# TensorE's order in the last three heads of an attention-decode block: the maxima of single heads before older value passes, the last group's turn before the last maxima

## The chip, the cores and the metric

The kernel runs on one core of a Trainium2 chip. The metric is device time in microseconds (us) of one launch. The engines are called PE (TensorE, matrix multiplication), DVE (VectorE), ACT (ScalarE), POOL (GpSimd) and SP (SyncE, which here only issues DMA transfers). Each engine works through its own list of instructions in order; between engines there are semaphores. A time printed as "at 638.5" is counted from the start of the span of the profiled execution.

## The reference, cut to what matters

One token passes through a transformer block whose layer norms are modulated by a vector `c`: attention over a cache of 16384 keys and values with 32 heads of 128, then a gated feed-forward network (FFN) with inner size 1728. The model width is 640. All inputs are bfloat16.

```python
mod = (silu(c) @ w_mod).reshape(1, 6, 1, 640)
sa, ca, ga, sb, cb, gb = (mod[:, i] for i in range(6))
h = layernorm(x) * (1 + ca) + sa
# attention A: Hq = Hkv = 32, Sk = 16384, Dh = 128
q = (h @ wq).reshape(1, 1, 32, 128)
scores = einsum('bhqd,bhkd->bhqk', q, k_cache) * 128 ** -0.5
p = softmax(scores)
o = einsum('bhqk,bhkd->bhqd', p, v_cache)
x = x + ga * (o.reshape(1, 1, 4096) @ wo)
# FFN B: F = 1728
h = layernorm(x) * (1 + cb) + sb
x = x + gb * ((silu(h @ w_gate) * (h @ w_up)) @ w_down)
```

The keys and the values are 32 x 4 MB each. They, `wo` and the FFN weights are read once, so about 290 MB pass from memory into the core.

## The kernel before, in words

**How operations get their order.** The kernel is written as a plan. Each operation is given an engine, a position (a number that looks like a time in us) and the operations it depends on. At the end every engine's operations are sorted by position and written out as that engine's list; where a dependency crosses engines a semaphore wait is put in front of the operation. A wait holds all that stands behind it on the same engine. DMA transfers are operations of SP, so their order is the order of positions on SP.

**Units.** Keys are treated in units (`UNITS`): 15 pairs of heads (units 0 to 14, heads 0 to 29), and then head 30 alone (unit 15) and head 31 alone (unit 16). `NU` is 15, `H` is 32. `BU(u)` and `EU(u)` are the planned begin and end of a unit: unit 15 has 614.0 and 632.6, unit 16 has 633.8 and 652.4. `B` and `E` in the loop stand for these; `TL` is `BU(16)`.

**Scores, on DVE.** For each unit DVE multiplies the keys in place with the broadcast query in two halves (L577, `mult`), adds halves together three times (L597, `fold`), reduces the rest to scores in `S_sb` (L599, `red`) and takes the maximum of each partition (L601, `max`, into `pm`).

**Maxima and softmax.** `stage_top` (L461) turns the partition maxima into one number. PE transposes `pm` into a row (L464, called row15 and row16 below for the last two units), DVE takes the maximum of the row (L466, top15 and top16), PE broadcasts it to all partitions (L474), and ACT scales it (L478, `nb`). `softmax` then has ACT write the exponentials (L496 for a single head, into `P_sb`). The two DVE steps of a unit's maximum stand in the DVE list between the two multiplications of the next unit: the list is mult of unit 16, first half; top15; mult of unit 16, second half; folds; red16; max16; top16.

**Values, on PE.** `value(h)` (L523) is one pass of 32 matmuls (L529) over the 4 MB of values of head `h`, called pv28, pv29 and pv30 below. It depends on the exponentials of that head and on the landing of its values. ACT copies the result into the head's four rows of `acc_sb` (L540). When all heads of a group are there, `diag` (L543, matmuls L547) turns the group's rows into columns; for the last group it is diag7 and covers heads 28, 29 and 30. Head 31 has another form: 128 small matmuls (L631, pv31 below), in three parts as its values land in three parts of 2, 1 and 1 MB. `sums` (L513) adds the exponentials and inverts the sum (L515 on PE, two ACT operations).

**Behind the heads.** The product with `wo` (L670) takes 155 small matmuls for heads 0 to 30 and five more for head 31; then come the residual and the second layer norm, `gate` and `up` (L733, 140 matmuls), `down` (L751, 70 matmuls in three parts as its weights land), and the output.

**SP's list at the end.** Values of head 30 (waits for pv28, whose slot of `vring` it takes), `wo` in three transfers, values of head 31 in three transfers (wait for pv29), then `w_gate`, `w_up` and five transfers of `w_down` (all wait for red16, since they take the slots of the last keys).

**PE's list at the end.** pv28; pv29; row15; the broadcast of top15; sums for heads 28 to 30; row16; the broadcast of top16; sums for head 31; pv30; diag7; `wo` for heads 0 to 30; pv31; and the rest as above.

## Time and profile before

| what | value |
|---|---|
| median of 3 runs | 692.49 us (692.16 to 694.05) |
| the profiled execution | 692.85 us |
| its span (first to last instruction) | 691.1 us |
| DVE busy | 612.9 us, 89% of the span |
| PE busy | 330.8 us, 48% of the span |
| ACT busy | 66.3 us, 10% of the span |
| memory read | 290.48 MB, 420 GB/s over the span |
| mean granted PE clock | 0.72 of full speed |

The span is what the profile's times refer to; the 1.75 us by which the profiled time is longer lie around it. The page gives for each engine its busy time; a view of stretches gives the same for any part of the span, with the granted clock and the busy share of the 16 DMA engines; the chain of waits follows the end of the span back, at each step to what released it; and the list of transfers gives for each issue the time until its data had landed.

### The profile page before, as it was taken

The page shows a single profiled execution, that of the slowest core. Times are in us where ns is not written, and L with a number is a line of the kernel's source. Part 1 is how long each engine was busy: PE and PEld are TensorE (multiplying, and loading weights), DVE is VectorE, ACT ScalarE, POOL GpSimd, SP SyncE. Part 2 cuts the span into 40 slices and gives each one's busy share as a digit, 9 for nine tenths or more (in the row PEclk, how much of TensorE's full clock was granted, in tenths as well). Part 3 has the DMA queues.
Part 4 walks back from the last instruction along what each step waited for, and adds up shares of the span by engine and source line. Part 5 has one row for each costly group of instructions (what it writes and reads, how often), then busy time and mean ns, then how long its engine had stood idle before and what let it go on. Part 6 is the DMA issues. An engine that isn't in the chain of part 4 may idle for free.

```text
span 691.1 us, 5975 instructions
## 1 busy us (share of the span) xinstructions
PE 330.8 (48%) x1946; PEld 137.7 (20%) x1946; DVE 612.9 (89%) x195; ACT 66.3 (10%) x210; POOL 0.2 (0%) x4
## 2 busy tenths in 40 slices
PE   2440270908164553719028644719082644737186
PEld 2210020303021111303003211203021211212056
DVE  3079999999999999999999999999999999996801
ACT  1020100001010101010011101010000101010000
POOL 0000000000000000000000000000000000000000
PEclk9985595867768685959559785958686775959565
DMA  9999999999999999999999999999999999999991
GB/s 394 417 442 425 436 439 425 458 403 448 421 436 424 465 408 427 451 421 432 424 438 434 450 408 429 453 419 439 421 459 412 450 413 435 430 427 417 417 415 64
DMA packets 11238, 290.68 MB, mean 421 GB/s; under 512 B 1046, under 2 KB 1752, under 8 KB 3928
## 3 DMA queue, kind: packets, MB, share of 16 engines
q1 hardware_dynamic: 11220, 290.48, 97.9%
q8 instruction: 10, 0.16, 0.1%
q14 instruction: 4, 0.03, 0.0%
q10 hardware_dynamic: 4, 0.00, 0.0%
HBM read 290.48 MB, written 0.00 MB: 420 GB/s over the span
## 4 chain that ended last, share of the span: by engine, by line
DMA 42%; DVE 36%; PE 20%; issue 1%; ACT 1%; SPq 0%; DVEq 0%
DMA vbig<-in_A_v_cache_dram 33%; PE psb L529 16%; DVE kbig L577 16%; DVE kbig L597 13%; DMA kbig<-in_A_k_cache_dram 5%; DMA x_row<-in_A_x_dram 4%; DVE S_sb L599 4%; DVE kbig L592 1%; PE psb L733 1%; PE psb L670 1%; PE psb L631 1%; ACT P_k L492 0%; PE psb L751 0%; DVE pm L601 0%; DVE gm L466 0%
## 5 line engine op out<-in xcount | busy, mean ns | idle before, releaser
L577 DVE TENSOR_TENSOR kbig<-kbig,qbc 128x8192 bf16<-128x8192 bf16 (+2 forms) x34 | 278.0, 8175 | 23.8 <-DMA kbig<-in_A_k_cache_dram 23.8
L529 PE MATMUL psb<-vbig,P_sb 128*4 128x512 bf16 (+1 forms) x992 | 258.1, 418 | 26.4 <-DMA vbig<-in_A_v_cache_dram 20.6
L597 DVE TENSOR_TENSOR kbig<-kbig 128x8192 bf16<-128x8192 bf16 (+3 forms) x50 | 238.3, 4766 | 1.7
L529 PEld LDWEIGHTS psb<-vbig,P_sb 128*4 128x4 bf16 (+1 forms) x992 | 88.2, 89 | 189.1 <-issue 85.3
L464 PE MATMUL psb<-ident_f,pm 128*1 128x128 f32 x34 | 9.6, 381 | 199.5 <-DVE pm L601 199.5
L599 DVE TENSOR_REDUCE S_sb<-kbig 128x256 f32<-128x4096 bf16 (+1 forms) x17 | 70.9, 4169 | 0.6
L540 ACT ACTIVATE acc_sb<-psb 4x512 f32<-4x512 f32 x31 | 18.2, 586 | 268.3 <-PE psb L529 268.3
L464 PEld LDWEIGHTS psb<-ident_f,pm 128*1 128x1 f32 x34 | 1.5, 81 | 204.5 <-DVE pm L601 204.2
L474 PE MATMUL psb<-gm,ones_f 1*64 1x1 f32 (+1 forms) x64 | 6.6, 254 | 57.3 <-DVE gm L466 57.3
L478 ACT ACTIVATE nb<-psb 128x1 f32<-128x1 f32 x17 | 2.9, 172 | 184.1 <-PE psb L474 183.9
L504 PE MATMUL psb<-P_k,place 128*128 128x128 bf16 x60 | 9.1, 308 | 22.9 <-ACT P_k L492 22.9
L474 PEld LDWEIGHTS psb<-gm,ones_f 1*64 1x64 f32 (+1 forms) x64 | 5.1, 203 | 63.5 <-DVE gm L466 63.5
L372 PE MATMUL psb<-vbig,h_col 128*128 128x512 bf16 x40 | 12.5, 484 | 10.0 <-DMA vbig<-in_A_wq_dram 10.0
L492 ACT ACTIVATE P_k<-S_sb,nb 64x256 bf16<-64x256 f32 x30 | 15.2, 506 | 0.9
L559 ACT ACTIVATE Z<-msk,on_f 128x16 bf16<-128x16 f32 (+1 forms) x28 | 6.4, 298 | 71.7 <-DVE on_f L554 71.7
L621 DVE TENSOR_TENSOR On<-psb,rl 128x3 bf16<-128x3 f32 x1 | 0.2, 165 | 13.0 <-PE psb L547 13.0
L547 PE MATMUL psb<-sel,acc_sb 128*128 128x4 f32 (+1 forms) x64 | 8.4, 255 | 5.4 <-ACT acc_sb L540 5.4
L466 DVE TENSOR_REDUCE gm<-psb 1x2 f32<-1x128 f32 (+1 forms) x17 | 4.6, 273 | 6.3 <-PE psb L464 6.3
L504 PEld LDWEIGHTS psb<-P_k,place 128*128 128x128 bf16 x60 | 5.2, 131 | 24.1 <-ACT P_k L492 24.1
L547 PEld LDWEIGHTS psb<-sel,acc_sb 128*128 128x128 f32 x64 | 7.7, 191 | 9.4 <-ACT acc_sb L540 9.4
L592 DVE TENSOR_TENSOR kbig<-kbig 128x8192 bf16<-128x8192 bf16 x2 | 8.8, 4424 | 0.1
L634 DVE TENSOR_TENSOR On<-psb,rl 128x1 bf16<-128x1 f32 x1 | 0.2, 160 | 9.7 <-PE psb L631 9.7
(96 smaller groups left out, 102.9 us busy)
## 6 DMA issues: line engine op xcount, KB each, us to landing
vbig<-in_A_v_cache_dram SPq DMA_DIRECT2D x31, 4096.0 KB, 29.3
kbig<-in_A_k_cache_dram SPq DMA_DIRECT2D x4, 4096.0 KB, 33.4
vbig<-in_A_wq_dram SPq DMA_DIRECT2D x1, 5120.0 KB, 25.7
kbig<-in_w_mod_dram SPq DMA_DIRECT2D x1, 4800.0 KB, 14.1
kbig<-in_A_wo_dram SPq DMA_DIRECT2D x1, 3840.0 KB, 22.5
kbig<-in_B_w_gate_dram SPq DMA_DIRECT2D x1, 2160.0 KB, 13.4
kbig<-in_B_w_up_dram SPq DMA_DIRECT2D x1, 2160.0 KB, 18.2
vbig<-in_A_v_cache_dram SPq DMA_DIRECT2D x1, 2048.0 KB, 18.3
```

The source lines that it names most:

```text
L372: last = e.matmul(q_ps[b][:, 0:n * 128], lhsT=h_col[:, k:k + 1].broadcast_to([128, 128]), rhs=wv[:, k, n0:n0 + n * 128], start=(k == 0), s ...
L464: o_T = op(PE, E + 0.1, lambda e: e.matmul(row_ps, lhsT=pm[:, u:u + 1], rhs=ident_f[:], start=True, stop=True), deps=[o_max[u], o_idf, lnl ...
L474: last = e.matmul(top_ps[w * hh:w * hh + w, :], lhsT=ones_f[0:1, 0:w], rhs=gm2[:, hh:hh + 1], start=True, stop=True)
L492: o_exp[h + hh] = op(ACT, pt + 0.2 + 0.01 * hh, lambda e, p_=p_, hh=hh: e.activation(out=P_k[p_], in_=S_sb[p_, :], func=ACTF.Exp, scale=SC ...
L504: last = e.matmul(R_ps[:, TT * hh:TT * (hh + 1)], lhsT=place[:, hh, eo, :], rhs=P_k[:, TT * eo:TT * (eo + 1)], start=(eo == 0), stop=(eo = ...
L529: return e.matmul(acc_ps[s2][0:4, :], lhsT=P_sb[:, s2, bass.ds(t, 4)], rhs=vbig[:, bass.ds(at, 512)], start=start, stop=stop)
L540: o_acc[h] = op(ACT, pos + 0.05, lambda e: e.activation(out=acc_sb[32 * j:32 * j + 4], in_=acc_ps[s2][0:4, :], func=ACTF.Copy), deps=[o_pv ...
L547: last = e.matmul(OT_ps[:, h0:h0 + n], lhsT=acc_sb[:, 128 * i:128 * (i + 1)], rhs=sel[:, i, 0:n], start=(i == 0), stop=(i == 3))
L577: prev.append(op(DVE, B + (13.0 if u == 0 else 4.5) * c, lambda e, ks=ks[:, a:b, :], qb=qb: e.tensor_tensor(out=ks, in0=ks, in1=qb, op=ALU ...
L592: prev[c] = op(DVE, B + 13.0 * c + 8.7, lambda e, ks=ks[:, a:b, :]: e.tensor_tensor(out=ks[:, :, 0:64], in0=ks[:, :, 0:64], in1=ks[:, :, 6 ...
L597: prev = [op(DVE, E - 14.0 + 0.1 * (8 - math.log2(w)), lambda e, ks=ks, w=w: e.tensor_tensor(out=ks[:, :, 0:w], in0=ks[:, :, 0:w], in1=ks[ ...
L599: o_red[u] = op(DVE, E - 4.0, lambda e, ks=ks, w=w, nt=nt: e.tensor_reduce(out=S_sb[:, 0:nt], in_=ks[:, :, 0:w], axis=AX.X, op=ALU.add), d ...
```

## The change

Three things are moved in the plan; no operation is added or removed.

- The value pass of head 29 takes position `E + 0.15` of unit 15, that is 632.75, where it had 618.7. Row15 stands at 632.7, so row15 now comes before pv29 in PE's list. The transfer of head 31's values, which waits for pv29, takes 633.1 where it had 620.2.
- The value pass of head 30 is placed at 638.3, directly behind the sums for heads 28 to 30, where it had 653.2. The transfer of its values keeps its position.
- diag7 takes `E + 0.15` of unit 16, that is 652.55, directly behind row16 (652.5) and before the broadcast of top16; it had 653.5.

PE's list at the end becomes: pv28; row15; pv29; the broadcast of top15; sums for heads 28 to 30; pv30; row16; diag7; the broadcast of top16; sums for head 31; `wo` for heads 0 to 30; pv31; and the rest as before. ACT's copies of the passes' results move with them: that of pv29 to 632.8, before `nb` of unit 15 as before, that of pv30 to 638.4, before `nb` of unit 16. The lists of DVE and SP keep their order.

```diff
@@ -583,11 +583,14 @@
                         value(hp, pt + 0.5)
                         if hp % GQ == GQ - 2:
                             sums(hp // GQ, pt + 0.6, hp - 2, GQ)
-                        value(hp + 1, pt + 0.7)
+                        value(hp + 1, pt + 0.7 if u < NU else E + 0.15)
                         if hp % GQ == GQ - 2:
                             diag(hp // GQ, pt + 0.8, hp - 2, GQ)
                     else:
                         sums(H, pt + 0.4, hp - 2, 3)
+                        load_v(hp, BU(NU) + 6.0)
+                        value(hp, pt + 0.5)
+                        diag(H // GQ - 1, E + 0.15, HD, H - 1 - HD)
...
         pt = softmax(NU + 1, EU(NU + 1) + 0.2)
-        load_v(H - 2, BU(NU) + 6.0)
         sums(H + 1, pt + 0.3, H - 1, 1)
-        value(H - 2, pt + 0.5)
-        diag(H // GQ - 1, pt + 0.8, HD, H - 1 - HD)
...
-        load_v(H - 1, BU(NU) + 6.2)
+        load_v(H - 1, EU(NU) + 0.5)
         s2 = (H - 1) % 2
```

## The prediction

> **What bounds the kernel now.** I read the chain of waits first, then the instructions in order of time over the last 100 us, then the stretches with the DMA share, then the transfers with their time to landing. The end of the chain, in columns start, length, what:

> ```profile
> 629.65 8.86 PE psb L529 x32
> 639.05 4.34 DVE kbig L577
> ...
> 653.78 0.30 DVE pm L601
> 654.12 0.60 PE psb L464 x2
> ...
> 657.02 9.22 PE psb L529 x32
> ...
> 667.96 4.10 PE psb L670 x155
> 672.07 0.51 PE psb L631 x19
> 672.57 2.17 issue
> 674.74 3.06 PE psb L631 x109
> ...
> 681.81 4.44 PE psb L733 x140
> 686.57 2.13 PE psb L751 x70
> ```

> Here the end is set by a dependency chain: pv29 (629.65 to 638.51), DVE's work on unit 16 until max16 (654.08), the softmax of head 31, pv30 (657.02 to 666.24), diag7, `wo`, pv31 with a pause of 2.17 us in which PE waited for nothing the profile shows, the second norm, gate and up, down. PE did next to nothing between 640.6 and 654, though pv30 could have run. DVE lost time too (start, length, engine, operation; in brackets the idle time before it and its releaser):

> ```profile
> 628.53 0.29 DVE L601 TENSOR_REDUCE pm<-S_sb 128x1 f32<-128x128 f32 x1
> ...
> 638.77 0.28 DVE L466 TENSOR_REDUCE gm<-psb 1x1 f32<-1x128 f32 x1 [5.61 <-PE psb L464]
> ```

> The partition maxima of head 30 were ready at 628.82, but row15 stood behind pv29, so top15, and behind it the second half of unit 16's multiplication, waited 5.61 us. Now the DMA side, as stretches (last two columns: busy share of the 16 DMA engines, GB/s):

> ```profile
> 638.00:654.00 16.00, 1.49 (x9) 0.76 (x7) 15.06 (x7) 1.63 (x6) 0.00 (x0) 0.59 1.02 419
> 654.00:662.00 8.00, 6.72 (x20) 2.64 (x21) 0.34 (x2) 1.04 (x5) 0.00 (x0) 0.53 0.99 411
> 668.00:672.00 4.00, 4.00 (x157) 4.00 (x154) 0.17 (x1) 0.00 (x0) 0.00 (x0) 0.54 1.02 412
> 672.00:676.00 4.00, 1.83 (x70) 1.77 (x68) 0.00 (x0) 0.00 (x0) 0.00 (x0) 0.50 1.04 391
> 676.00:678.00 2.00, 1.78 (x67) 1.70 (x64) 0.17 (x2) 0.00 (x0) 0.00 (x0) 0.50 0.33 112
> ```

> The DMA engines are full until 676 and done at 678: a second bound, close behind the first. The transfers give its landings (KB each, us from issue to landing):

> ```profile
> vbig<-in_A_v_cache_dram SPq DMA_DIRECT2D x1, 4096.0 KB, 13.6
> vbig<-in_A_v_cache_dram SPq DMA_DIRECT2D x1, 2048.0 KB, 18.3
> kbig<-in_B_w_gate_dram SPq DMA_DIRECT2D x1, 2160.0 KB, 13.4
> kbig<-in_B_w_up_dram SPq DMA_DIRECT2D x1, 2160.0 KB, 18.2
> kbig<-in_B_w_down_dram SPq DMA_DIRECT2D x1, 80.0 KB, 11.2
> ```

> With the issue times from the instructions in order of time (625.74, 638.54, 653.77, 654.19, 666.8): head 30's values land at 639.3; head 31's first half at 656.8 and its last quarter, issued at 639.9 with a median of 21.1 for the two quarters, near 661.8; w_gate at 667.2, w_up at 672.4, and the last piece of w_down at 678.0. Before, down began at 686.57, so all of this had landed 8.5 us early.

> **The change, part by part.** No instruction is added or removed; only waits move.

> (1) *Row15 ahead of pv29.* It may start at 628.87 (max15 ends at 628.82) and takes 0.58 us, as row16 did on an idle PE: done at 629.45. Pv29 waited for its values until 629.65 anyway, so the cost is 0, hidden by that landing. If max15 came later, each us would hold pv29, its copy, the broadcast of top15, and SP's transfer of head 31 with all FFN weights behind it; the cover is 0.2 us. A later issue of head 31's values would still cost no DMA time until the engines ran out of `wo`, whose last piece lands 24.2 us after its issue at 627.1, at 651.

> (2) *DVE.* top15 no longer waits: first half until 633.16, top15, second half until 637.8, folds 8.0 us, red16 (waits for head 30's exponentials, part 3, long done) and max16 end 5.6 us earlier, at 648.5. SP may issue the FFN weights at 648.2, not 653.77.

> (3) *Pv30 ahead of row16.* The broadcast of top15 still stands behind pv29: 638.55 to 638.95. ACT copies pv29's result until 639.15 as before, then `nb` 0.17 and the exponentials with their sum 0.5: 639.9. Sums on PE 0.4: 640.3. Head 30's values landed at 639.3, so pv30 starts at 640.35. Its length: 8.0 us (all at full clock, the pass at 591.1 to 599.1) to 13.7 us (32 matmuls at 0.427, the spacing at half clock). I take 9.2, the pass of before, since PE idles about 1 us between the passes: end at 649.6. The granted clock fell to 0.50 in the long pause before pv30 (0.50 from 642 to 654), so a colder start is possible. [...]

> (4) *Row16, diag7, the last softmax.* Row16 waits for PE, not for max16: 649.6 to 650.2. The copy of pv30 takes 0.59, diag7 1.05: 651.3. Top16 (0.28) runs on DVE beside diag7. Broadcast 0.58, `nb` 0.2, exponentials 0.5, sums 0.58: 653.3. Diag7 before the broadcast costs 0.8 us here and saves its 1.05 later. `wo` (4.1 to 4.2 us; weights there since 651): 657.5. Pv31 needs 0.51 + 3.06, and I keep the 2.17 us pause: 663.2, past the last landing of head 31 (661.8). Before, pv31 ended at 677.80; this chain is 14.6 us shorter. The way on to gate takes 4.0 us (677.80 to 681.81): gate at 667.2, just when w_gate lands.

> (5) *What takes over.* The transfers do not move. The same packets go through engines that were full from 626 to 676, in the same order on SP; issuing the FFN weights 5.6 us earlier only lengthens the queue. So w_up lands at 672.4, up needs half of 4.44: 674.6, the product 0.33: 674.95. The first two parts of down fit in before the last piece of w_down at 678.0. Then the last 20 of 70 matmuls, 2.13 x 20 / 70 = 0.61, with 0.05 to react: 678.66. From the end of down (688.70) to the end of the span (691.07) it took 2.37: span **681.05**, 10.0 us less than before. The chain of part 4 may be 4.7 us late (gate at 671.9) before it decides again.

> The profiled time is 1.78 above its span and 0.36 above the median of the runs: 681.05 + 1.78 - 0.36 = **682.5**.

> **Rivals.**

> *B. PE's chain still decides.* Pv30 wholly at half clock adds 4.5 us (13.7 for 9.2) and one more pause like the 2.17 us one, in gate or pv31 while DMA is full, makes 6.7; less the slack of 4.7 leaves 2.0: 684.5 (683.7 to 687). For it: the clock stood at 0.50 in most of the tail, and the pause was real. Against: pv29 runs directly before, and passes back to back took 8.0.

> *C. The transfers end sooner.* If the earlier issue let them finish 4.2 us sooner, the whole 14.6 would be gained: 692.5 - 14.6 = 677.9. Against: shares of 0.99 to 1.04 leave no hole to fill.

> *D. Slower: FFN weights share the queue with head 31.* They are now issued 13 us before head 31's last quarter lands, before it was 8. If the engines served them side by side, head 31's values would land only with everything else at 678.0; then the 128 matmuls, 0.51 + 3.06, end pv31 at 681.6 and the old way of 13.27 (677.80 to 691.07) follows: 694.9, time 696.3. It decides against the change once the first half lands after 674.2 (677.80 - 3.57). Against: w_gate was already issued while head 31 was pending, yet the landings kept the order of issue, w_up 5.2 us behind w_gate (2.2 MB at 420 GB/s). [...]

> *E. The edit does nothing:* pv30 or row15 finds a wait that I overlooked and the old chain stands, 692.5. Both inputs, max15 at 628.82 and head 30's landing at 639.3, speak against it.

> **How the numbers follow.** My forecast has 0.78, B 0.12, C 0.04, D 0.04, E 0.02. The forecast's own range is 681.6 to 683.6 (the last landing within 0.5 us either way, and 0.5 for a new set of runs, whose spread before was -0.3 to +1.6). Towards C I go down to 681.0, towards B up to 685.2, which takes in half of B; beyond lie about 0.18. A measurement can tell about 0.3% (2.1 us) from no change. Faster: 0.78 + 0.12 + 0.04 = 0.94; same: 0.02; slower: 0.04.

> **What would show it.** Right: row15 at 628.9 and pv29 still at 629.7; top15 with no wait; max16 at 648.5; pv30 from 640.4; w_up's landing near 672.4 as before; up waiting for a DMA, and the last part of down starting at the last landing, near 678. Wrong: a DMA share clearly under 1 between 626 and 676, a landing of head 31 later than 662, gate later than 671.9, or pauses on PE between 657 and 676 that sum to over 5 us.

## The result, and the profile after

The changed kernel takes 684.44 us in the median of 4 runs (684.22 to 684.49), the kernel before 692.65 in the same comparison: ratio 0.9878, 95% interval 0.986 to 0.9895. It is 8.2 us faster, where 10.0 had been forecast. Its profiled execution took 684.22 with a span of 682.4, 8.6 less than the span before. The forecast of 682.5 was 1.9 us too low; the range (681.0 to 685.2) holds the result.

The instructions of the changed kernel in order of time; columns start, length, engine, line, operation, and in brackets the idle time before it and what ended it. Lines between the two edits have moved by three, so L604 is the maximum that was L601:

```profile
628.73 0.58 PE L464 MATMUL psb<-ident_f,pm 128*1 128x128 f32 x2 [2.44 <-DVE pm L604]
629.49 8.33 PE L529 MATMUL psb<-vbig,P_sb 128*4 128x512 bf16 x32 [0.18 <-DMA vbig<-in_A_v_cache_dram]
632.92 0.27 DVE L466 TENSOR_REDUCE gm<-psb 1x1 f32<-1x128 f32 x1
...
639.53 7.81 PE L529 MATMUL psb<-vbig,P_sb 128*4 128x512 bf16 x32
...
647.92 0.29 DVE L604 TENSOR_REDUCE pm<-S_sb 128x1 f32<-128x128 f32 x1
...
650.97 3.77 PE L670 MATMUL psb<-A_sb,kbig 128*128 128x1 bf16 x140
...
657.55 1.87 PE L631 MATMUL psb<-P_sb,vbig 128*128 128x1 bf16 x64 [2.41 <-DMA vbig<-in_A_v_cache_dram]
...
662.38 1.01 PE L631 MATMUL psb<-P_sb,vbig 128*128 128x1 bf16 x32 [1.49 <-DMA vbig<-in_A_v_cache_dram]
...
667.82 2.31 PE L733 MATMUL psb<-h_col,kbig 128*128 128x1 bf16 x70 [1.45 <-DMA kbig<-in_B_w_gate_dram]
...
673.00 2.25 PE L733 MATMUL psb<-h_col,kbig 128*128 128x1 bf16 x70 [2.88 <-DMA kbig<-in_B_w_up_dram]
...
679.27 0.78 PE L751 MATMUL psb<-gu_col,kbig 128*128 128x1 bf16 x20 [0.71 <-DMA kbig<-in_B_w_down_dram]
```

Read it from the top: row15 runs before pv29, and pv29 still starts with its values; top15 starts without a wait; pv30 has moved from 657 to 639.5. From 657 on every long block of matmuls is released by a transfer; in the profile before, pv31, gate, up and down never waited for one. PE's chain arrives early everywhere and waits for data. PE's waits by releaser (total us, times, longest) say the same in one view:

```profile
PE psb L631 <- DMA vbig<-in_A_v_cache_dram: 4.4, 3, 2.4
PE psb L733 <- DMA kbig<-in_B_w_up_dram: 2.9, 1, 2.9
PE psb L751 <- DMA kbig<-in_B_w_down_dram: 2.4, 3, 1.1
PE psb L733 <- DMA kbig<-in_B_w_gate_dram: 1.4, 1, 1.4
```

So the end is set by the last landing. And that landing is later than before. The transfers after (KB, us from issue to landing; issued at 647.92, 648.34 and, the last, 667.40):

```profile
kbig<-in_B_w_gate_dram SPq DMA_DIRECT2D x1, 2160.0 KB, 19.8
kbig<-in_B_w_up_dram SPq DMA_DIRECT2D x1, 2160.0 KB, 24.6
...
kbig<-in_B_w_down_dram SPq DMA_DIRECT2D x1, 80.0 KB, 11.8
```

The landings are 667.7, 673.0 and 679.2; before they were 667.1, 672.4 and 678.0. Up to `wo` the changed kernel is 0.15 ahead (wo's last landing 651.80 for 651.95), so the same bytes in the same order lost 1.34 us between 652 and 679. The stretches show that the engines were not idle (last two columns: DMA share, GB/s):

```profile
655.00:660.00 5.00, 2.13 (x74) 1.96 (x71) 0.00 (x0) 0.00 (x0) 0.00 (x0) 0.50 1.00 413
...
670.00:676.00 6.00, 2.37 (x73) 2.19 (x71) 0.76 (x4) 0.18 (x1) 0.00 (x0) 0.50 1.03 403
676.00:677.00 1.00, 0.68 (x26) 0.71 (x27) 0.00 (x0) 0.00 (x0) 0.00 (x0) 0.50 0.74 263
677.00:678.00 1.00, 0.39 (x15) 0.31 (x13) 0.00 (x0) 0.00 (x0) 0.00 (x0) 0.50 0.30 97
678.00:679.50 1.50, 0.79 (x28) 0.71 (x27) 0.00 (x0) 0.00 (x0) 0.00 (x0) 0.50 0.03 12
```

The engines are full to 676 (shares 1.00 to 1.03) and then run out one after another; a share of 0.03 of 16 engines from 678 on means that on average half an engine was still busy. The last landing waits for what finishes late: of the 48 completions of the last three transfers, 16 each, the first is at 676.02, the third last at 678.60 and the last two at 679.02 and 679.22. (In e8 and e10 below, where the last piece's completions can be told from the others, one engine completes it 1.5 and 0.9 us behind the next.) What made the end late is the question of the second half of the experiments.

The trace also has the times at which each of the 16 engines completed its share of a transfer. For the first half of head 31's values (us from the start of the span, sorted):

```
before  655.13 655.28 655.29 655.29 655.30 655.34 655.35 655.38 656.05 656.15 656.16 656.41 656.48 656.70 656.71 656.84
after   655.62 655.63 655.68 655.80 655.89 656.17 656.20 656.20 656.22 656.29 656.38 656.52 656.58 656.66 656.73 657.50
```

Before there are two groups of eight, and nobody alone. After, one engine stands 0.77 behind all others. The trace doesn't number the engines, and how they are spread differs from run to run from the start; what can be compared is the order within one run. What else was moved at the time is the second DMA row of the page, instructions in blocks of 16 KB ("q8 instruction": packets, MB, share; 10 packets, 0.16 MB in the whole span). That they are PE's is seen from e5 to e7, where 256 and 512 PE instructions more bring one and two blocks more, and some 620 fewer bring two less (from 640 on: five blocks in e5 and two in e7, for four in the changed kernel). Between 640 and 676, before:

```profile
q8 instruction: 2, 0.03, 0.4%
```

and after:

```profile
q8 instruction: 3, 0.05, 0.6%
```

After, the blocks were fetched at 655.3, 661.5, 672.0 and 677.4; before, at 672.1 and 675.9, and at 682.8 and 686.7 when the transfers were over. PE reached its long unrolled sequences (`wo`, pv31, gate, up: 428 matmuls, two instructions each, a weight load and the matmul) 11 to 17 us earlier, and so three of the four blocks are fetched while the engines are full.

### The profile page after: what moved, and what is told of

Its sections match the earlier page's. It is cut to its first block, busy times and chain, and to the rows that moved or that the text cites. A ratio compares the mean times of both kernels' runs of the same rounds, so it can differ in the third digit from the quotient of the medians.

```text
span 682.4 us, 5973 instructions
## 1 busy us (share of the span) xinstructions
PE 329.8 (48%) x1944; PEld 137.1 (20%) x1946; DVE 612.9 (90%) x195; ACT 66.2 (10%) x210; POOL 0.2 (0%) x4
## 4 chain that ended last, share of the span: by engine, by line
DVE 67%; DMA 23%; PE 6%; SPq 3%; ACT 1%; issue 1%
DVE kbig L577 31%; DVE kbig L600 26%; DMA kbig<-in_A_k_cache_dram 17%; DVE S_sb L602 8%; PE psb L529 5%; DMA x_row<-in_A_x_dram 4%; SPq L71 3%; DMA kbig<-in_B_w_down_dram 2%; DVE kbig L595 1%; DVE pm L604 0%; DVE gm L466 0%; ACT P_k L492 0%; PE psb L504 0%; PE psb L547 0%; PE psb L751 0%
## 5 line engine op out<-in xcount | busy, mean ns | idle before, releaser
L577 DVE TENSOR_TENSOR kbig<-kbig,qbc 128x8192 bf16<-128x8192 bf16 (+2 forms) x34 | 278.0, 8175 | 23.3 <-DMA kbig<-in_A_k_cache_dram 23.3
L529 PE MATMUL psb<-vbig,P_sb 128*4 128x512 bf16 (+1 forms) x992 | 258.6, 418 | 22.1 <-DMA vbig<-in_A_v_cache_dram 15.9
L529 PEld LDWEIGHTS psb<-vbig,P_sb 128*4 128x4 bf16 (+1 forms) x992 | 88.0, 89 | 185.5 <-issue 88.1
L464 PE MATMUL psb<-ident_f,pm 128*1 128x128 f32 x34 | 9.5, 380 | 189.7 <-DVE pm L604 189.7
L464 PEld LDWEIGHTS psb<-ident_f,pm 128*1 128x1 f32 x34 | 1.4, 80 | 195.1 <-DVE pm L604 195.1
L372 PE MATMUL psb<-vbig,h_col 128*128 128x512 bf16 x38 | 10.8, 449 | 10.6 <-DMA vbig<-in_A_wq_dram 10.4
L634 DVE TENSOR_TENSOR On<-psb,rl 128x1 bf16<-128x1 f32 x1 | 0.2, 160 | 13.6 <-PE psb L631 13.6
L381 ACT ACTIVATE qbc<-psb 64x256 bf16<-64x256 f32 (+1 forms) x16 | 5.8, 364 | 23.2 <-PE psb L372 23.1
## 6 DMA issues: line engine op xcount, KB each, us to landing
vbig<-in_A_v_cache_dram SPq DMA_DIRECT2D x31, 4096.0 KB, 28.7
kbig<-in_A_k_cache_dram SPq DMA_DIRECT2D x4, 4096.0 KB, 33.4
kbig<-in_B_w_gate_dram SPq DMA_DIRECT2D x1, 2160.0 KB, 19.8
kbig<-in_B_w_up_dram SPq DMA_DIRECT2D x1, 2160.0 KB, 24.6
vbig<-in_A_v_cache_dram SPq DMA_DIRECT2D x1, 2048.0 KB, 19.7
```

Of the source, the lines that this page charges most:

```text
L464: o_T = op(PE, E + 0.1, lambda e: e.matmul(row_ps, lhsT=pm[:, u:u + 1], rhs=ident_f[:], start=True, stop=True), deps=[o_max[u], o_idf, lnl ...
L529: return e.matmul(acc_ps[s2][0:4, :], lhsT=P_sb[:, s2, bass.ds(t, 4)], rhs=vbig[:, bass.ds(at, 512)], start=start, stop=stop)
L577: prev.append(op(DVE, B + (13.0 if u == 0 else 4.5) * c, lambda e, ks=ks[:, a:b, :], qb=qb: e.tensor_tensor(out=ks, in0=ks, in1=qb, op=ALU ...
```

## The experiments

From the forecast stood T, that the end is the later of PE's chain and of the last landing plus about 3.2 us, and against it several rivals, in which PE's chain decides or the parts add up. F is the theory on the late engine: each block of PE instructions delays the one engine that fetches it. G, its rival, says that the later landing is scatter.

**Only row15 first (e1).** From the kernel before:

```diff
-                        value(hp + 1, pt + 0.7)
+                        value(hp + 1, pt + 0.7 if u < NU else E + 0.15)
...
-        load_v(H - 1, BU(NU) + 6.2)
+        load_v(H - 1, EU(NU) + 0.5)
```

> Only the first part of the change: row15 ahead of head 29's value pass; head 30's pass and diag7 stay where they were. Theory T (the end is the later of PE's chain and the last FFN landing plus about 3.2 us): DVE gains 5.6 us, pv30 still stands behind the last softmax, so the old chain ends 5.6 us earlier and still decides: span 685.5, time about 687, gate near 676.2 with no wait for a transfer. Rival R1 (the transfers already decide in this form too): about 684.4, with gate, up or down waiting for transfers. Rival R2 (the gain came from pv30 alone, DVE's 5.6 us go elsewhere): 692.6, no change.

Measured: 687.33 (ratio to the kernel before 0.9926, 0.9909 to 0.9942), span 685.7. The end of the chain of waits (start, length, what):

```profile
651.39 9.72 PE psb L529 x32
...
667.40 1.93 issue
669.33 3.06 PE psb L631 x109
...
676.40 4.44 PE psb L733 x140
```

T holds to 0.3 us: gate at 676.4 with no wait for a transfer (the last weights landed at 678.3, down began at 681.2). This part alone is worth 5.4 us, DVE's wait.

**Only pv30 first (e2).** From the kernel before:

```diff
                         sums(H, pt + 0.4, hp - 2, 3)
+                        load_v(hp, BU(NU) + 6.0)
+                        value(hp, pt + 0.5)
...
-        load_v(H - 2, BU(NU) + 6.0)
         sums(H + 1, pt + 0.3, H - 1, 1)
-        value(H - 2, pt + 0.5)
```

> Only the second part: head 30's value pass ahead of row16; row15 stays behind head 29's pass and diag7 behind the last sums, FFN weights are issued at 653.8 as before. Theory T: max16 at 654.1 as before, wo from about 657 to 661.3, pv31 until about 665 to 667, gate at 669 to 671, which is still before 671.9, so the last landing decides and the time is that of the whole change, 684.4 within 0.8. Rival R1 (parts add up: 8.2 in all, 5.6 of it by the first part): about 689.8. Rival R2 (FFN weights issued earlier are what helped): close to 692.

Measured: 685.35 (684.53 to 686.33; ratio 0.9903, 0.9887 to 0.992), just outside the 0.8 allowed. The parts do not add up: 5.4 and 7.3 alone, 8.2 together. In the chain of waits of this run's profile:

```profile
662.50 1.94 issue
664.44 3.06 PE psb L631 x109
...
671.51 4.33 PE psb L733 x138
675.84 1.80 issue
677.64 0.28 PE psb L733 x2
```

This profile is of the fastest of the four runs. PE's chain and the last landing (679.2) end almost together here. Down ran without a wait from 678.25 to 680.37, 0.35 later than the landing would have allowed. It met two pauses, of 1.9 and 1.8 us, on the way, where the expectation had room for one. They lie exactly 256 matmuls apart (109, 5 for head 31's `wo`, 2 and 2 in the norm, 138), that is 512 instructions, and blocks were fetched at 662.0 and 675.2, 0.5 to 0.7 us before each pause. A third block, at 668.1, was fetched while PE went through the norm, and there is no pause. From 662.0 by 668.1 to 675.2 are two blocks, so 256 instructions make one. So the pauses called "issue" go with block fetches; that PE outruns them is a reading of this, not a measurement.

**diag7 back (e3).** From the changed kernel, diag7 behind the last sums again:

```diff
-                        diag(H // GQ - 1, E + 0.15, HD, H - 1 - HD)
...
         sums(H + 1, pt + 0.3, H - 1, 1)
+        diag(H // GQ - 1, pt + 0.8, HD, H - 1 - HD)
```

> The whole change without its third part: diag7 back behind the last sums. Theory T: PE's chain gets 0.2 to 1.1 us longer ahead of wo, all of it inside the wait for head 31's values (pv31 stands 2.4 us waiting for the first of them): 684.4 within 0.3. Rival (PE's chain decides): 684.7 to 685.5.

Measured: 684.22 (684.16 to 684.38), the changed kernel's time. The third part is worth nothing here, as PE stands still before pv31 in both forms (2.4 us for head 31's first half, in each).

**Without the transfer of w_up (e4).** From the changed kernel:

```diff
-        d_wu = plan.dma(TW + 0.01, wu_v, ..., "wu", deps=wdeps, name="dma_wu")
+        d_wu = d_wg
```

> The changed kernel without the transfer of w_up (2.2 MB; up multiplies with what lies in the buffer, so up's part of the output is left out). Theory T: all later landings move 5.3 us forward, the last from 679.2 to about 673.9; up runs directly behind gate; down ends about 0.8 after the last landing; span about 677.1, time about 679. Rival (PE's chain decides, transfers only fill its gaps): no more than 0.5 us gained, 684.

Measured: 681.12 (two runs, 680.69 and 681.54), span 679.7. 3.3 us gained, where T had 5.3 and its rival 0.5. The last landing did come 4.8 us earlier, at 674.4. But up now ran directly behind gate and met a pause of 2.14 us called "issue", and PE's chain decided again (instructions in order of time):

```profile
668.17 4.30 PE L733 MATMUL psb<-h_col,kbig 128*128 128x1 bf16 x138 [1.55 <-DMA kbig<-in_B_w_gate_dram]
674.62 0.27 PE L733 MATMUL psb<-h_col,kbig 128*64 128x1 bf16 x2 [2.14 <-issue]
675.22 2.12 PE L751 MATMUL psb<-gu_col,kbig 128*128 128x1 bf16 x70 [0.34 <-DVE gu_col L742]
```

The expectation lacked the 2.14 us: by the landing alone (674.42, then 0.05, 0.78 and 2.39) the span would have been 677.6, and it was 679.7. T's direction stands, and this pause is a second limit close behind.

**128 more matmuls before pv31 (e5).** From the changed kernel:

```diff
+        def f_pad(e):
+            last = None
+            for i in range(128):
+                last = e.matmul(A_ps[:, 400:401], lhsT=ident[:], rhs=ones_bf[:, 0:1], start=True, stop=True)
+            return last
+        op(PE, TL + 29.49, f_pad, deps=[o_ident, o_ones, o_pn], name="pad")
```

> The changed kernel with 128 more small matmuls on PE (into an unused column) between wo and pv31, where PE waits 2.4 us for head 31's values. That is 256 more instructions, one more 16 KB block of PE's instruction stream. Theory F (each block is fetched by one of the 16 DMA engines and delays that engine's share of the weights by about 1.6 us; a transfer lands with its slowest engine): five blocks are fetched from 640 on and not four; pv31 ends 1 to 4 us later, inside the slack; the last part of w_down lands between 0 and 1.6 us later than 679.2, depending on whether the hit engine was a late one: time 684.4 to 686. Rival G (fetches are harmless; the transfers' end at 679.2 is only scatter): the landing stays within 0.3 of 679.2 and no single engine completes far behind the others.

Measured: 684.35 (683.97 to 685.05). Five blocks were fetched from 640 on (655.7, 661.7, 667.8, 674.7, 678.4), as F has it. The weights of up landed with one engine alone at 673.70, 1.06 behind the next, against G; but the last landing was 679.18, as without the added work, so the time can't tell F from G. PE's three pauses (1.57, 2.38 and 1.35 us; 128 matmuls lie between the first and the second, 256 between the second and the third) and the added work used up its slack: down ran from 677.84 to 680.01 with hardly a wait.

**256 more matmuls in the idle time of the kernel before (e6).** The same function with `range(256)` at position 640.0 in the kernel before.

> The kernel before with 256 more small matmuls on PE (into an unused column) in its idle time from 641 on, that is two more instruction blocks while the transfers are full. Theory F: two more fetches between 641 and 654, with pauses of about 2 us each on PE among the added matmuls; at the landing of head 31's first half (656.8 before, where the 16 engines complete without an outlier between 655.1 and 656.8) two engines have moved back by about 1.6 us, to 656.7 to 658.5; the time does not move (692.5 within 0.8), since the chain and not the transfers decides there. Rival G: the 16 completions lie as before.

Measured: 692.69 (ratio 0.9998, 0.9988 to 1.0009): no difference in time, as both theories say. The completions tell them apart. Blocks were fetched at 645.0 and 651.4. PE paused once among the added matmuls, for 1.99 us from 645.6, where two pauses had been expected; at the second fetch it had no more of them to run. Sorted completions, with a bar where the early engines end:

```
before, wo's last part          650.22 ... 650.48 (8) | 651.16 ... 651.95 (8)
e6,     head 30's values        637.15 ... 637.72 (8) | 638.74 ... 639.44 (8)
e6,     wo's last part          649.79 ... 650.35 (7) | 651.37 ... 652.08 (9)
before, head 31's first half    655.13 ... 655.38 (8) | 656.05 ... 656.84 (8)
e6,     head 31's first half    654.68 ... 655.25 (6) | 656.26 ... 656.96 (10)
```

After each fetch one engine fewer is in the early group. This can be followed through all twelve profiles, for each two successive transfers from head 30's values to the first part of w_down. Where no block is fetched between the two, the 16 sorted completions keep their spacing to 0.2 us, nearly always to 0.1. Where one is fetched (28 times), they don't, but one entry can be left out of each list so that the other fifteen keep theirs to 0.1, and the one left out comes 1.5 to 1.7 us late (once 1.9). In e6, for example, the one at 637.72 is 1.56 late in `wo`'s first part. That is F: one engine is delayed by each fetch, and a slowing of all engines by PE's work would not look like this.

Whether the last landing moves depends on which engine is hit. In the kernel before, the fetch at 672.1 hit the second of the 16; it moved to 674.92, just behind the next at 674.80, and the last landing was 678.03. In the changed kernel the fetch at 672.0 hit the thirteenth, which became the last by 0.78, and the last landing was 679.22. In e6 the block that stood at 672.1 before came at 671.1 and hit the eleventh: the last landing was 679.21, though PE's chain and the order of transfers were those of the kernel before. It did not show in the time, since the chain ends later there.

**PE's last stage thinned out (e7).** From the changed kernel:

```diff
+        wo_seq = [(k, g) for k, g in wo_seq if k == 0 or k >= 24]
...
-                for t in range(VSPLIT[c], VSPLIT[c + 1]):
+                for t in [t for t in range(VSPLIT[c], VSPLIT[c + 1]) if t % 4 == 0 or t == TT - 1]:
...
-            for j in range(FCH):
+            for j in range(4):
```

> The changed kernel with PE's last stage thinned out: the product with wo leaves out heads 1 to 23, pv31 takes every fourth tile of values and the last one, and gate and up compute only the first 4 of 14 column blocks (the rest stay zero). All transfers stay. Some 620 instructions fewer, about 2.4 blocks. Theory F: one or two blocks and not four are fetched from 640 on; the last part of w_down lands near 678.0 as before the change (up to 1.6 later if a late engine is hit), down ends 0.8 after it: span 681.2 to 682, time near 683. Rival G (the landing at 679.2 has nothing to do with fetches): landing 679.2, time 684.4. Rival R (PE's work decides): over 4 us less, since gate and up are 3.2 us shorter and pv31 and wo 6.

Measured: 683.26 (683.05 to 683.60), span 681.3: 1.2 us less than the changed kernel, and no more, though PE has some 310 matmuls less to do. The difference is 0.2%, but the four runs lie apart from all runs of the changed kernel (684.21 to 684.49 in two sets). The instruction row between 640 and 676 and the end of down:

```profile
q8 instruction: 1, 0.02, 0.2%
```

```profile
676.59 0.69 PE L752 MATMUL psb<-gu_col,kbig 128*128 128x1 bf16 x20 [0.77 <-DMA kbig<-in_B_w_down_dram]
678.09 0.79 PE L752 MATMUL psb<-gu_col,kbig 128*128 128x1 bf16 x20 [0.81 <-DMA kbig<-in_B_w_down_dram]
```

One block, at 655.5, and it hit an early engine (eight early at head 31's first half, seven at w_down's first part); one more came at 677.7, when the engines had nearly run out. The last landing is 678.05, that of the kernel before (678.03). G falls, with e6: the transfers are the same, and the landing goes with the fetches. R, that PE's work decides, falls with it.

The eleven profiles that move all the bytes agree. In three of them (before, e1, e7) every block fetched up to 675.2 hit one of the first eight engines in the order of completion, and the last landing was 678.03 to 678.33. In the eight others at least one hit an engine of the last eight, and the last landing was 679.18 to 679.65. (Fetches after 675.2 can't be followed in this way, as the engines run out.) One of the eight is e2, where the FFN weights were issued 5 us later than in the changed kernel (652.9 for 647.9), so their earlier issue is not the cause. E7 speaks against the forecast's rival D too: the FFN weights were issued as early as in the changed kernel, and head 31's first half landed at 656.75 (656.84 before).

**A version meant to be faster (e8, and again e10 beside e9, the changed kernel).**

```diff
-        WD_CUTS = [0, 6, 2 * NP2 - 2]
+        WD_CUTS = [0, 6, 2 * NP2 - 2, NF]
```

> A version meant to be faster: the changed kernel with down's last part cut once more, so that only 5 matmuls (the last 64 rows of w_down) and not 20 stand behind the last landing. Theory T (the last landing decides, and 20 matmuls take 0.78 us behind it): 0.4 to 0.6 us less, 683.9. Rival (something behind the landing decides): no change from 684.4.

> The changed kernel once more, as the measure for the next run on the same chip: 684.4 within 0.3, four blocks of PE instructions fetched from 640 on, the last part of w_down landing 0 to 1.6 us later than 678.0 because one engine is late.

> The version with down's last part cut once more, on the same chip as the run before it. Theory T with F: 0.3 to 0.6 us less than the changed kernel in the median where the last two pieces land apart, nothing where one late engine lands both together. Rival: no difference.

Measured: e8 683.82 (683.77 to 684.47), e9 684.26, and beside it e10 684.36. The 0.6 us of e8 did not come back where the two ran on the same chip: no gain is shown. The profile of e10 says why: the late engine completes the piece before the last at 679.45 and the last, smaller piece at 679.65, so down's last 20 matmuls still run in one go:

```profile
679.50 0.79 PE L751 MATMUL psb<-gu_col,kbig 128*128 128x1 bf16 x20 [0.50 <-DMA kbig<-in_B_w_down_dram]
```

## Why the prediction was right, and where it was off

*Row15 ahead of pv29 at no cost*: right. Row15 ran from 628.73, pv29 from 629.49, released by its values.

*DVE gains 5.6 us*: right. Max16 ended at 648.2 (648.5 forecast); e1 shows this part alone as 5.4 us of time.

*Pv30 in 9.2 us*: too long. It ran from 639.5 to 647.3, 7.8 us, all at full clock (granted 1.00 from 639.5 to 647.4). In the 1.7 us between the end of pv29 and pv30, in which PE had two short steps, the granted clock stayed at 1.00 (637.8 to 639.5).

*The last softmax and `wo`*: `wo` was done at 655.1 (657.5 forecast), nearly all of it because pv30 had ended at 647.3 and not at 649.6.

*Pv31 with its pause of 2.17*: the pause did not show. PE waited for head 31's values at that point anyway, and the block came in meanwhile (fetched at 655.3, values at 657.5). What looked like a property of pv31 is one of block boundaries, as e2, e4 and e5 show. These errors of the chain, pv30 and the pause, fell into slack and cost the forecast nothing; the time does not test them.

*The transfers take over*: right, and this is why 14.6 us of shorter chain became 8.6 of span. E1 and e2 show that either part alone brings most of it.

*"The transfers do not move"*: this is the step that failed. It took the last landing as fixed at 678.0, since the data packets, their order and the full engines are the same. It counted only the data queue. The instruction blocks, which the page lists as a queue of 0.1%, were pulled into the full time along with PE's work, and what waits for a transfer waits for the last of its 16 completions (pv31 began at 657.55, the last of head 31's first half came at 657.50 and the one before at 656.73). The last landing measured 679.22; in e7, with one block that hit an early engine, it is back at 678.05. The remaining terms: 20 matmuls behind the landing took 0.78 for 0.61 (70 in a row took 2.12 before: by these two, 50 matmuls more add 1.34, 27 ns each, so 20 of 70 are not 20/70 of the time), and the way to the end 2.39 for 2.37. In all 1.22 + 0.17 + 0.02 = 1.41 of span, counted from 681.03, to which the forecast's terms add up (it says 681.05). The step from span to median adds 0.58: the profiled run lay 0.36 above its median before and 0.22 below it after. Together this is 1.99, and less the 0.05 that the forecast was rounded up (681.05 for 681.03, 682.5 for 682.47) it is the 1.94 missed. Two more figures of the forecast are slightly off without an effect: `wo`'s last part landed at 651.95 before, not 651, and by its own terms gate could start as late as 671.8, not 671.9.

*Rivals*: B did not happen in the whole change but nearly in e2. C would have needed earlier landings, and they were later. D did not happen: the larger transfers landed in the order of their issue in every profile. In the changed kernel head 31's three parts landed at 657.50, 659.83 and 662.34, w_gate at 667.68 and w_up at 672.96. What mattered instead is how far the engines of one transfer finish apart: its completions are spread over 1.1 us (wo's last part in the changed kernel) to 3.9 us (w_down's first part in e8).

Open: what decides which engine fetches a block. Whether the last landing moved hung on that, and the profile before could not tell which one it would be. In both profiles of the changed kernel the last landing was 679.2, so it may not be pure chance. Nor is it tried how the unrolled sequences could be made shorter without leaving work out.

## What to carry to other kernels

When a chain is shortened under full transfers, look first at the landing times: here they were the floor, and parts that each gained alone didn't add up on it (5.4 and 7.3 gave 8.2). Take the floor from the slowest of the 16 engines and count what else they carry; here one instruction block of 16 KB that hit a late engine cost 1.2 us, and another that hit an early one cost nothing. A pause that no engine explains, in a long unrolled sequence, may go with such a fetch: compare its place with the fetches, and with the next pause (256 instructions on in e5, 512 in e2).

## What was not expected of the hardware

PE waited 1.35 to 2.4 us when it ran matmuls of 28 ns each (109 of pv31 in 3.06 us) under full transfers (2.17 in before, 1.93 in e1, 1.94 and 1.80 in e2, 2.14 in e4, 1.57, 2.38 and 1.35 in e5, 1.99 and 2.19 in e6; a part may be hidden behind another wait). Where the fetches are given, each such wait began within 1.2 us of one: at 672.57 in before, with the fetch at 672.1; in e5 at 656.5, 661.7 and 675.9, with fetches at 655.7, 661.7 and 674.7. PE showed no pause where it was slow or waiting when the block was fetched (655.3, 661.5 and 672.0 in the changed kernel, 668.1 in e2), and none in the kernel before at the fetches of 675.9, 682.8 and 686.7, when it ran such matmuls but the transfers were running out or over. That the state of the transfers makes this difference is not tested.
